# Routing logits placed one unit of work later, and the forms of five experts' weights moved by 3 to 7 work steps

## The chip, the core and the metric

The kernel runs on one core of one Trainium2 chip. The metric is the device time of one execution in microseconds (us); lower is better. Engines are named as in the profile: PE (matmul), PEld (its weight load), DVE (vector), ACT (scalar), POOL (GpSimd) and SP, which here only issues DMAs.

## What is computed

Two blocks follow each other. A sketched attention (batch 4, 4 heads, 1088 tokens, head size 32) gives x with 4352 rows of 128 columns; a mixture of 8 experts, weighted by Sinkhorn routing, works on x:

```python
logits = x @ w_gate                    # 4352 x 8
P = np.exp(logits - logits.max())
for _ in range(8):
    P /= P.sum(1, keepdims=True) + 1e-09
    P /= P.sum(0, keepdims=True) + 1e-09
    P *= N / E
for e in range(E):
    h = np.maximum(x @ w1[e], 0.0)     # 128 -> 1024
    ye = h @ w2[e]                     # 1024 -> 128
    out += P[:, e:e + 1] * ye
```

## The kernel before

**x, in four quarters.** x is kept transposed in `xT`, one quarter of 1088 columns for each batch. The quarter of batch 3 comes last: DVE makes it, `take_over` (L559) writes it to DRAM (`xd`) and reads it back into `xT`, the first 192 of each 288 columns through POOL's DMA queue, the rest through SP's. The last DMAs of both queues are noted in `last_moves`.

**Work steps.** Expert work needs only the quarters that are there, so it starts while attention still runs. `steps()` (L1621) is a generator; each of its steps makes one tile of hidden units (two matmuls, L1147, and their relu on ACT, L1151), issues DVE's differences of older tiles (L1166) and PE's second products (L1601) that are due; tiles are multiplied 8 steps after the first of their block. `fill(n)` (L1713) runs steps until n units are used up; a step costs its columns over 480 units, 416/480 = 0.867 in steps 49 to 96 and 384/480 = 0.8 from 97 on. What stands between two `fill`s in `routing()` (L679) goes to the engines at that place. In this part PE, DVE and ACT run strictly in program order, and all relu tiles, the logits and the small routing products share four PSUM banks in turn (`bank`, L88).

**Routing.** It starts after step 63. `logits(c)` (L573) multiplies the gate with one chunk of columns (512, 288, 288) of all four quarters: four matmuls, each on 32 columns of the PE array, the last for batch 3. `logits_turned` transposes a chunk on DVE, L693 takes the maximum, the matmul L697 turns it, ACT makes the exponentials (L702). Each of eight Sinkhorn iterations is a run of small DVE operations (L708 to L714), one PE product (L718) and two more DVE operations; then `pT` is stored (L730), and weighted sources `xe` and `de` (L862, L876) are made from its parts `px` for the long middle part, which begins at about 199 us.

**Forms.** For experts 1 to 7 the middle part needs sums and differences of quarters of `w1`, made ahead and kept in DRAM as `wl` and `wf`. `forms_ahead(e, area)` (L267) gives nine pieces: 1 five loads on SP, two from DRAM to DRAM (`raw_of_first`, L265) and three into SBUF called d, t3 and z (L279); 2 d is negated on ACT (L282) and a second load is added to it by an accumulating DMA on POOL (L276); 3 the same for t3; 4 the lower half of z is negated; 5 the upper half of z is made on ACT from the summed d; 6 d's lower half is copied out (SP, L279); 7 z is added to d (POOL); 8 two copies out; 9 the last copy out, of the new d. `forms_at` (L595) hangs piece i on the work step that has the number of `passed` at the call plus its i-th figure. Experts 1 and 2 are placed earlier (`forms_of_two`, after step 48) and still have pieces at steps 64 to 75; experts 3 to 7 are placed by `forms_of_five` (L604), after step 63. SP and POOL issue these DMAs in program order, so one that waits holds the later ones.

Groups of columns change after steps 64, 80, 96 and 112; four to eight steps later ACT copies the finished sums out of PSUM (L954 to L971, nine copies).

Of the kernel before, what the change touches and what calls it, by code (L numbers as in the profile page):

```python
# [44 lines left out]
def kernel(  # L45
# [12 lines left out]
    nc = tc.nc  # L58
    P = nc.NUM_PARTITIONS
    B, H, S, D = q.shape  # L60
# [27 lines left out]
    def bank():  # L88
        return aps.tile([P, 512], F32, tag="a", name="a")
# [29 lines left out]
    xT = big.tile([P, N + 2 * 32], F32, name="xT")  # L119
# [132 lines left out]

    fast = {}

    def split(t):

        return t.rearrange("p (k b f) -> p k b f", k=2, b=2)

    def raw_of_first(e):

        w = fast[e][0]
        for out, x in ((w[upper], moe_w1[e][upper]), (split(w)[lower, :, 0], split(moe_w1[e])[lower, :, 0])):
            tc.keep_in_program_order(nc.sync.dma_start(out=out, in_=x))  # L265

    def forms_ahead(e, area):  # L267

        w = split(moe_w1[e])
        fast[e] = [dram.tile([P, F], F32, name=f"{n}{e}") for n in ("wl", "wf")]  # L270
        wl, wf = (split(t) for t in fast[e])
        d, t3, z = (x.rearrange("p (k f) -> p k f", k=2) for x in area)
        t3 = t3[lower]

        def plus(out, x):
            tc.keep_in_program_order(nc.gpsimd.dma_start(out=out, in_=x, accum_op=Alu.add))  # L276

        def copied(queue, out, x):
            tc.keep_in_program_order(queue.dma_start(out=out, in_=x))  # L279

        def turn(out, x):
            nc.scalar.activation(out=out, in_=x, func=Act.Copy, scale=-1.0)  # L282

        def loads():
            if nc.sync in last_moves:
                with tc.issue_after(last_moves.pop(nc.sync).ins):
                    raw_of_first(e)
            else:
                raw_of_first(e)
            copied(nc.sync, d, w[:, :, 0])  # L290
            copied(nc.sync, t3, w[lower, :, 1])
            copied(nc.sync, z[lower], w[upper, :, 1])

        def turn_all():
            turn(area[0], area[0])
            plus(area[0], w[:, :, 1])

        def turn_low():
            turn(area[1][lower], area[1][lower])
            plus(t3, w[upper, :, 1])  # L300

        def turn_lowest():
            turn(area[2][lower], area[2][lower])

        def turn_across():
            turn(area[2][upper], area[0][lower])

        def keep_low():
            copied(nc.sync, wf[lower, :, 0], d[lower])

        def last_sum():
            plus(area[0], area[2])

        def keep_two():
            copied(nc.sync, wl[lower, :, 1], t3)
            copied(nc.sync, wf[upper, :, 0], z[upper])

        def keep_rest():
            copied(nc.sync, wf[:, :, 1], d)

        return loads, turn_all, turn_low, turn_lowest, turn_across, keep_low, last_sum, keep_two, keep_rest

    wd = consts.tile([P, 2, H, R], F32, name="wd")
# [35 lines left out]
    wg = consts.tile([P, 32], F32, name="wg")  # L359
# [197 lines left out]
    last_moves = {}  # L557
# [15 lines left out]
    def logits(c):  # L573
        lo, hi = chunks[c]
        pg = bank()[:, 0:hi - lo]
        for b in range(B):
            nc.tensor.matmul(pg[32 * b:32 * (b + 1)], wg, xT[:, b * S + lo:b * S + hi], start=True, stop=True,
                             tile_position=(0, 32 * b))
        lgs.append((c, pg))

    lgs = []
# [1 line left out]
    def logits_turned():  # L583
        c, pg = lgs.pop(0)
        lo, hi = chunks[c]
        nc.vector.transpose(out=lgp[:, lo // 32:hi // 32, :].rearrange("p a e -> p (a e)"), in_=pg)

    def pieces(t, n):
        t = t.rearrange("p a b -> p (a b)") if len(t.shape) == 3 else t.rearrange("p a b c -> p (a b c)")
        return [t[:, F // 2 * i:F // 2 * (i + 1)] for i in range(n)]  # L590

    v_left = [pieces(t, 2) for t in v_slots]
    ph_left = [pieces(t, 4) for t in phs]

    def forms_at(e, area, *steps_):  # L595
        for at_, do in zip(steps_, forms_ahead(e, area)):
            aside.setdefault(passed[0] + at_, []).append(do)
# [6 lines left out]
    def forms_of_five():  # L604
        kp = pieces(wk.tile([P, (NT + 1) * H, R, R], F32, tag="kp", name="kp", bufs=1), 4)
        r = pieces(rb, 4)
        forms_at(3, [ph_left[0][3], v_left[0][1], kp[0]], 1, 10, 11, 12, 16, 17, 20, 21, 25)
        forms_at(4, kp[1:4], 6, 13, 14, 15, 19, 20, 23, 24, 28)
        forms_at(5, r[0:3], 12, 17, 18, 20, 26, 27, 30, 31, 35)
        forms_at(6, ph_left[1][0:3], 19, 27, 28, 29, 33, 34, 37, 38, 42)  # L610
        forms_at(7, [r[3], ph_left[1][3], v_left[1][0]], 25, 30, 31, 32, 36, 37, 39, 40, 44)

    def attention(b):

# [64 lines left out]
    def routing():  # L679

        forms_of_five()
        yield 5
        logits(0)
        logits(1)
        yield 0.5
        logits_turned()
        logits(2)
        yield 0.5
        logits_turned()
        logits_turned()  # L690
        lg = lgp[:, :, 0:E]
        mx = sk.tile([P, 1], F32, tag="mx", name="mx")
        nc.vector.tensor_reduce(out=mx, in_=lg, axis=AX.XY, op=Alu.max)  # L693
        yield 3
        pm = bank()[:, 0:P]
        for s in range(2):
            nc.tensor.matmul(pm[64 * s:64 * (s + 1)], mx.to_broadcast([P, 64]), ident, start=True, stop=True,  # L697
                             tile_position=(0, 64 * s))
        nc.vector.reduce_max(mx, pm, axis=AX.X)
        nc.vector.tensor_scalar(mx, mx, -1.0, 64 * math.log(2.0), op0=Alu.mult, op1=Alu.add)  # L700
        pw = p2s[0]
        nc.scalar.activation(out=pw[:, :, 0:E], in_=lg, func=Act.Exp, bias=mx[:, 0:1])  # L702

        step = 1.5 * 2.0 ** (23 - 149 + 64)
        nc.vector.tensor_scalar(pw[:, :, 0:E], pw[:, :, 0:E], step, step, op0=Alu.add, op1=Alu.subtract)
        for it in range(ITERS):
            rs = sk.tile([P, SA], F32, tag="rs", name="rs")
            nc.vector.reduce_sum(rs, pw, axis=AX.X)  # L708
            nc.vector.reciprocal(rs, rs)
            p1 = p1s[it % 2]  # L710
            nc.vector.scalar_tensor_tensor(p1[:, 0:SA], rs.unsqueeze(2).to_broadcast([P, SA, E]), UP,
                                           pw[:, :, 0:E], op0=Alu.mult, op1=Alu.mult)
            cs = sk.tile([P, E], F32, tag="cs", name="cs")
            nc.vector.reduce_sum(cs, p1.rearrange("p g e -> p e g"), axis=AX.X)  # L714
            yield 4.25
            pc = bank()[:, 0:E]
            for s in range(2):
                nc.tensor.matmul(pc[64 * s:64 * (s + 1)], ones[:, 0:64], cs, start=True, stop=True,  # L718
                                 tile_position=(0, 64 * s))
            cr = sk.tile([P, E], F32, tag="cr", name="cr")  # L720
            nc.vector.reciprocal(cr, pc)
            last = it == ITERS - 1
            pw = lgp if last else p2s[(it + 1) % 2]
            nc.vector.scalar_tensor_tensor(pw[:, :, 0:E], cr.unsqueeze(1).to_broadcast([P, SA, E]),
                                           float(N) / E * (1.0 if last else UP), p1[:, 0:SA],
                                           op0=Alu.mult, op1=Alu.mult)

        nc.vector.transpose(out=lgT.rearrange("p a s -> p (a s)"), in_=lgp.rearrange("p a e -> p (a e)"))
        for b in (1, 0, 2, 3):
            tc.keep_in_program_order((nc.gpsimd if b != 1 else nc.sync).dma_start(  # L730
                out=pT[:, b * S:(b + 1) * S], in_=lgT[32 * b:32 * b + E].rearrange("p a s -> p (a s)")))
# [564 lines left out]
    def middle():  # L1296
# [149 lines left out]
        def second_product(k, i, row):  # L1446
# [3 lines left out]
            for w, x, *place in products[k][i]:  # L1450
# [9 lines left out]
                if op is not None:  # L1460
                    tc.add_manual_dep(mm.ins, op, SYNC, reason="row tiles of one bank")
            waited[1 - row].discard(bank_)
# [1 line left out]

        products, witnesses, issued, waited = {}, [(0, last_relu[0])], [], (set(), set())
        written = {(i, row): -1 for i in range(4) for row in range(2)}
        SYNC = mybir.DependencyInfo(mybir.DependencyClass.Sync, mybir.DependencyReason.DATA)
        number = {}

        def witness(k, p, n, ins):  # L1470
# [18 lines left out]
        for n, k in enumerate(ks):  # L1489
# [3 lines left out]
            g, e = items[j]  # L1493
# [326 lines left out]
```

## Time and profile before

| what | value |
|---|---|
| three runs | 886.57, 886.80, 888.33 us; median 886.8 |
| the profiled execution | 886.74 us |
| its span, first to last instruction | 885.0 us, so 1.74 us lie around it |
| busy: PE, DVE, ACT, POOL | 876.4, 792.2, 570.7, 176.6 us |
| granted PE clock | 0.999 |
| DMA | 174.67 MB, mean 197 GB/s |

The times of the trace are counted from the first instruction. A row of the timeline gives start, length, engine, line, operation, output and inputs, how many instructions were merged (x4), and in brackets how long the engine was idle before and what ended that. SPq rows are DMA issues, not transfers.

### The profile page before, as it was taken

How to read it: one execution, taken by the hardware profiler on the slowest of the kernel's cores; microseconds unless marked ns; L12 is line 12 of the kernel's file. 1: busy time of each engine (PE TensorE's matmuls, PEld its weight loads, DVE VectorE, ACT ScalarE, POOL GpSimd, SP SyncE). 2: the span in 40 equal slices, each digit the busy share in tenths (PEclk: the TensorE clock that was granted, in tenths of full speed). 3: DMA queues.
4: the chain of work that ended last, by engine and by line, in shares of the span. 5: the costliest groups of instructions: out<-in, count | busy, mean ns of one | idle time of the engine just before them, and what ended most of it. 6: DMA issues, size and time to landing. Idle time of an engine off the chain costs nothing.

```text
span 885.0 us, 28699 instructions
## 1 busy us (share of the span) xinstructions
PE 876.4 (99%) x11790; PEld 628.1 (71%) x11790; DVE 792.2 (90%) x1628; ACT 570.7 (64%) x1309; POOL 176.6 (20%) x244
## 2 busy tenths in 40 slices
PE   9999999999999999999999999999999999999997
PEld 6777544454777777777777777888778777776665
DVE  7678778978999999999999999899998999998875
ACT  3356577678666677667676766676766666755643
POOL 3121333120211221222122211231122122200000
PEclk9999999999999999999999999999999999999999
DMA  9998799475877877877786777697568776774340
GB/s 258 305 278 276 160 228 213 108 180 176 235 220 208 244 217 205 235 185 209 197 240 172 212 212 191 168 241 219 173 165 227 212 226 179 208 203 97 94 106 13
DMA packets 97459, 174.67 MB, mean 197 GB/s; under 512 B 29216, under 2 KB 68976, under 8 KB 92480
## 3 DMA queue, kind: packets, MB, share of 16 engines
q1 hardware_dynamic: 74832, 139.67, 49.9%
q0 software_dynamic: 21264, 33.00, 21.6%
q8 instruction: 93, 1.52, 0.7%
q10 hardware_dynamic: 1232, 0.16, 0.1%
q14 instruction: 38, 0.31, 0.1%
HBM read 125.70 MB, written 25.08 MB: 170 GB/s over the span
## 4 chain that ended last, share of the span: by engine, by line
PE 90%; DVE 6%; ACT 1%; DMA 1%; issue 1%; SPq 0%; DVEq 0%; POOL 0%; POOLq 0%
PE s L1601 39%; PE a L1313 37%; PE a L1147 10%; DVE hb L1166 2%; PE a L421 1%; DVE hb L1215 1%; PE a L536 1%; PE a L108 1%; DMA xT<-xd 0%; PE a L388 0%; DVE hx L1215 0%; DVE ws L238 0%; PE s L450 0%; DMA xd<-xt 0%; ACT hb L1151 0%
## 5 line engine op out<-in xcount | busy, mean ns | idle before, releaser
L1313 PE MATMUL a<-xe,w 64*64 64x384 f32 x2164 | 418.1, 484 | 0.0
L1601 PE MATMUL s<-hb,ws 64*64 64x256 f32 (+4 forms) x2962 | 381.8, 384 | 1.1 <-DVE hb L1166 0.9
L1601 PE MATMUL s<-hx,ws 64*64 64x256 f32 (+1 forms) x2894 | 349.3, 376 | 0.1
L1313 PE MATMUL a<-de,w 64*64 64x384 f32 x1600 | 309.4, 483 | 0.0
L1601 PEld LDWEIGHTS s<-hb,ws 64*64 64x64 f32 (+1 forms) x2962 | 202.7, 133 | 73.7 <-issue 23.8
L1601 PEld LDWEIGHTS s<-hx,ws 64*64 64x64 f32 (+1 forms) x2894 | 196.9, 133 | 56.1 <-issue 10.2
L1215 DVE TENSOR_TENSOR hb<-hb 128x512 f32<-128x512 f32 (+1 forms) x340 | 187.7, 578 | 1.4 <-ACT hb L1348 1.1
L1313 PEld LDWEIGHTS a<-xe,w 64*64 64x64 f32 x2164 | 147.3, 133 | 25.4 <-issue 2.0
L1348 ACT ACTIVATE hx<-a 128x384 f32<-128x384 f32 x204 | 97.0, 492 | 63.9 <-PE a L1313 62.1
L1348 ACT ACTIVATE hb<-a 128x384 f32<-128x384 f32 x204 | 97.6, 492 | 59.5 <-PE a L1313 57.7
L1147 PE MATMUL a<-xT,w 128*64 128x256 f32 (+3 forms) x576 | 130.6, 453 | 0.4 <-ACT hb L1151 0.4
L1313 PEld LDWEIGHTS a<-de,w 64*64 64x64 f32 x1600 | 111.4, 133 | 19.2 <-ACT hb L1348 0.6
L1215 DVE TENSOR_TENSOR hx<-hx 128x512 f32<-128x512 f32 (+1 forms) x204 | 118.3, 595 | 0.0
L876 POOL DMA_DIRECT2D de<-xe x68 | 56.9, 984 | 295.2 <-ACT de L869 169.7
L1151 ACT ACTIVATE hb<-a 128x256 f32<-128x256 f32 (+3 forms) x148 | 66.6, 453 | 54.8 <-PE a L1147 44.5
L1344 ACT ACTIVATE hb<-a 128x384 f32<-128x384 f32 x136 | 66.7, 491 | 33.1 <-PE a L1313 31.9
L1353 DVE TENSOR_TENSOR a<-a,hb 128x384 f32<-128x384 f32 x136 | 76.7, 564 | 11.2 <-PE a L1313 7.0
L1342 ACT COPY a<-a 128x384 f32<-128x384 f32 x136 | 63.1, 464 | 31.5 <-PE a L1313 30.9
L1166 DVE TENSOR_TENSOR hb<-hb 128x416 f32<-128x416 f32 (+7 forms) x90 | 60.8, 675 | 21.2 <-ACT hb L1151 18.5
L1147 PEld LDWEIGHTS a<-xT,w 128*64 128x64 f32 x576 | 55.7, 137 | 28.0 <-issue 16.1
L1601 PE MATMUL s<-hb,w 128*64 128x256 f32 (+3 forms) x280 | 69.6, 435 | 0.0
L876 POOL DMA_DIRECT2D de<-de x34 | 29.6, 872 | 135.0 <-issue 78.1
(226 smaller groups left out, 1020.2 us busy)
## 6 DMA issues: line engine op xcount, KB each, us to landing
ws<-ws SPq DMA_DIRECT2D x34, 1280.0 KB, 6.5
w<-wl SPq DMA_DIRECT2D x34, 512.0 KB, 7.7
w<-wf SPq DMA_DIRECT2D x33, 512.0 KB, 8.3
px<-pT SPq DMA_DIRECT2D x34, 384.0 KB, 9.3
w<-in_moe_w_dram SPq DMA_DIRECT2D x16, 512.0 KB, 4.5
de<-xe POOLq DMA_DIRECT2D x34, 192.0 KB, 3.1
de<-de POOLq DMA_DIRECT2D x34, 192.0 KB, 8.1
ws<-in_moe_w_dram SPq DMA_DIRECT2D x7, 512.0 KB, 7.8
```

The costliest lines, as they stand in the source:

```text
L108: nc.tensor.matmul(warm[:, 0:P], ones, ones, start=True, stop=True)
L876: tc.keep_in_program_order(nc.gpsimd.dma_start(out=out, in_=x, accum_op=Alu.add))
L1147: nc.tensor.matmul(ph[sl], loaded_w[j][0][:, P * f + H2 * s:P * f + H2 * (s + 1)], sources[j][:, lo:hi], start=True, stop=True, tile_posit ...
L1151: last_relu[:] = [nc.scalar.activation(out=out, in_=ph, func=Act.Relu).ins.name]
L1166: nc.vector.tensor_tensor(out, a, b, op=Alu.subtract)
L1215: nc.vector.tensor_tensor(places(out), places(a), places(b), op=Alu.subtract if off else Alu.add)
L1313: nc.tensor.matmul(out[sl], w[r, c0 + H2 * s:c0 + H2 * (s + 1)], x[r], start=start, stop=stop, tile_position=(H2 * row, H2 * s), skip_grou ...
L1342: witness(k, p, 1, nc.scalar.copy(b, bx))
L1344: witness(k, p, 5, nc.scalar.activation(out=m5s[p], in_=b, func=Act.Copy, scale=1.0 if p else -1.0))
L1348: ins = nc.scalar.activation(out=out, in_=x, func=Act.Relu)
L1353: ins = nc.vector.tensor_tensor(by if what == 1 else raw(k, p, 1, 1), bb[p], m5s[p], op=Alu.add)
L1601: mm = nc.tensor.matmul(sums[g][i][H2 * s:H2 * (s + 1), n * place:n * (place + 1)], w, x, start=c == (2 if t == 3 and row is None else 1) ...
```

## The change

Three edits. `routing()` yields 6 units instead of 5 before the first two logits, and 2.25 instead of 3 before the maximum is turned. The last matmul of `logits(0)` is noted in `all_there`, and the first load of forms issued after it (expert 3's) waits for it by an added semaphore dependency. The five lines of `forms_of_five` have other steps. What was tied behind the last move of `xT` on SP was expert 3's first load; now it is the first copy out that SP issues for the forms after that move.

```diff
 in raw_of_first(e):
-            tc.keep_in_program_order(nc.sync.dma_start(out=out, in_=x))
+            ins = tc.keep_in_program_order(nc.sync.dma_start(out=out, in_=x))
+            if all_there:
+                tc.add_manual_dep(ins.ins, all_there.pop(), SYNC, reason="behind the last x")
 in forms_ahead:
         def copied(queue, out, x):
-            tc.keep_in_program_order(queue.dma_start(out=out, in_=x))
+            if queue in last_moves:
+                with tc.issue_after(last_moves.pop(queue).ins):
+                    queue.dma_start(out=out, in_=x)
+            else:
+                tc.keep_in_program_order(queue.dma_start(out=out, in_=x))
         def loads():
-            if nc.sync in last_moves:
-                with tc.issue_after(last_moves.pop(nc.sync).ins):
-                    raw_of_first(e)
-            else:
-                raw_of_first(e)
+            raw_of_first(e)
 in logits(c):
+        if c == 0:
+            all_there.append(mm.ins.name)
 in forms_of_five:
-        forms_at(3, [...], 1, 10, 11, 12, 16, 17, 20, 21, 25)
-        forms_at(4, [...], 6, 13, 14, 15, 19, 20, 23, 24, 28)
-        forms_at(5, [...], 12, 17, 18, 20, 26, 27, 30, 31, 35)
-        forms_at(6, [...], 19, 27, 28, 29, 33, 34, 37, 38, 42)
-        forms_at(7, [...], 25, 30, 31, 32, 36, 37, 39, 40, 44)
+        forms_at(3, [...], 8, 13, 14, 15, 19, 20, 23, 24, 28)
+        forms_at(4, [...], 11, 16, 17, 18, 26, 27, 30, 31, 35)
+        forms_at(5, [...], 15, 20, 21, 27, 31, 32, 35, 36, 40)
+        forms_at(6, [...], 20, 28, 29, 30, 34, 35, 38, 39, 43)
+        forms_at(7, [...], 26, 32, 33, 35, 42, 43, 46, 47, 50)
 in routing:
-        yield 5
+        yield 6
         logits(0)
         logits(1)
 ...
-        yield 3
+        yield 2.25
         pm = bank()[:, 0:P]
```

Counting the units gives the places, as the number of steps done:

| what | before | after |
|---|---|---|
| logits 0 and 1 | 69 | 70 |
| logits 2, first chunk turned | 70 | 71 |
| other chunks turned, maximum | 70 | 72 |
| maximum turned by PE, exponentials | 74 | 74 |
| products of the eight iterations | 79, 84, 89, 93, 99, 104, 109, 114 | 79, 84, 89, 94, 99, 104, 109, 115 |
| pieces 1 to 9 of expert 3 | 64, 73, 74, 75, 79, 80, 83, 84, 88 | 71, 76, 77, 78, 82, 83, 86, 87, 91 |
| of expert 4 | 69, 76, 77, 78, 82, 83, 86, 87, 91 | 74, 79, 80, 81, 89, 90, 93, 94, 98 |
| of expert 5 | 75, 80, 81, 83, 89, 90, 93, 94, 98 | 78, 83, 84, 90, 94, 95, 98, 99, 103 |
| of expert 6 | 82, 90, 91, 92, 96, 97, 100, 101, 105 | 83, 91, 92, 93, 97, 98, 101, 102, 106 |
| of expert 7 | 88, 93, 94, 95, 99, 100, 102, 103, 107 | 89, 95, 96, 98, 105, 106, 109, 110, 113 |

Left as they are: expert 1's pieces 7, 8, 9 at steps 64, 65, 69, and expert 2's pieces 5 to 9 at 66, 67, 70, 71, 75.

More of the change, by code (lines that the diff above doesn't have):

```diff
@@ L251, in store_four @@
         tc.keep_in_program_order(nc.sync.dma_start(out=stored_four[e], in_=ws))
-    fast = {}
+    fast, all_there = {}, []
+    SYNC = mybir.DependencyInfo(mybir.DependencyClass.Sync, mybir.DependencyReason.DATA)
     def split(t):
@@ L576, in logits @@
         for b in range(B):
-            nc.tensor.matmul(pg[32 * b:32 * (b + 1)], wg, xT[:, b * S + lo:b * S + hi], start=True, stop=True,
-                             tile_position=(0, 32 * b))
+            mm = nc.tensor.matmul(pg[32 * b:32 * (b + 1)], wg, xT[:, b * S + lo:b * S + hi], start=True, stop=True,
+                                  tile_position=(0, 32 * b))
+        if c == 0:
+            all_there.append(mm.ins.name)
         lgs.append((c, pg))
@@ L606, in forms_of_five @@
         r = pieces(rb, 4)
[L607 to L611, printed above, removed]
+        forms_at(3, [ph_left[0][3], v_left[0][1], kp[0]], 8, 13, 14, 15, 19, 20, 23, 24, 28)
+        forms_at(4, kp[1:4], 11, 16, 17, 18, 26, 27, 30, 31, 35)
+        forms_at(5, r[0:3], 15, 20, 21, 27, 31, 32, 35, 36, 40)
+        forms_at(6, ph_left[1][0:3], 20, 28, 29, 30, 34, 35, 38, 39, 43)
+        forms_at(7, [r[3], ph_left[1][3], v_left[1][0]], 26, 32, 33, 35, 42, 43, 46, 47, 50)
     def attention(b):
@@ L1466, in middle @@
         written = {(i, row): -1 for i in range(4) for row in range(2)}
-        SYNC = mybir.DependencyInfo(mybir.DependencyClass.Sync, mybir.DependencyReason.DATA)
         number = {}
```

## Prediction

> **What bounds the kernel now.** First the page's head, then the waits of PE over the whole run.
>
> ```profile
> span 885.0 us, 28699 instructions
> PE 876.4 (99%) x11790; PEld 628.1 (71%) x11790; DVE 792.2 (90%) x1628; ACT 570.7 (64%) x1309; POOL 176.6 (20%) x244
> PE 90%; DVE 6%; ACT 1%; DMA 1%; issue 1%; SPq 0%; DVEq 0%; POOL 0%; POOLq 0%
> ```
> ```profile
> PE s L1601 <- DVE hb L1166: 0.9, 2, 0.7
> PE a L577 <- DMA xT<-xd: 0.7, 1, 0.7
> PE a L1147 <- ACT hb L1151: 0.4, 1, 0.4
> ```
>
> PE is busy for 876.4 of 885.0 us and owns 90% of the chain. The change issues the same PE products, so it can only win or lose in PE's waits. Three of the kinds of wait fall where the edits are, 2.0 us of idle PE together. I then read PE's timeline around them.
>
> ```profile
> 106.10 1.06 PE L577 MATMUL a<-xT,wg 128*32 128x512 f32 x6
> 107.81 1.50 PE L577 MATMUL a<-xT,wg 128*32 128x512 f32 x10 [0.66 <-DMA xT<-xd]
> 109.25 0.92 PE L1147 MATMUL a<-xT,w 128*64 128x416 f32 x4
> 110.00 0.87 PE L1601 MATMUL s<-hb,w 128*64 128x416 f32 x4
> 110.80 0.69 PE L577 MATMUL a<-xT,wg 128*32 128x288 f32 x8
> 111.42 0.92 PE L1147 MATMUL a<-xT,w 128*64 128x416 f32 x4
> ...
> 113.56 0.51 PE L1601 MATMUL s<-hb,ws 128*64 128x416 f32 x1
> ...
> 113.91 0.51 PE L1601 MATMUL s<-hb,ws 128*64 128x416 f32 x1
> ```
> ```profile
> 130.63 0.92 PE L1147 MATMUL a<-xT,w 128*64 128x416 f32 x4 [0.43 <-ACT hb L1151]
> 142.85 0.56 PE L1601 MATMUL s<-hb,ws 128*64 128x416 f32 x1 [0.71 <-DVE hb L1166]
> ```
>
> The reader is to see that an idle time understates its loss. A matmul of 416 columns is shown 0.51 long, but the next starts 0.35 after it; what the two overlap, 0.16, is lost as well when PE has to wait. **Wait A**, the logits: three quarters ran (x6, two records each), the fourth waited for its part of xT, and the two chunks filled 106.10 to 109.25, 3.15 us. Chunk 2, with all four quarters side by side, took 110.80 to 111.42, 0.62 for 288 columns; at that rate 512 + 288 columns take 1.72. The loss is 1.43, twice the idle. **Wait B** (130.63): 0.43 + 0.16 less a little pipeline, 0.55. **Wait C** (142.85): 0.71 + 0.16 = 0.87.
>
> What is behind B and C stands in the timelines of ACT, SP, POOL and DVE:
>
> ```profile
> 128.63 0.63 ACT L282 ACTIVATE rb<-rb 128x512 f32<-128x512 f32 x1 [3.46 <-DMA rb<-in_moe_w_dram]
> 129.16 0.50 ACT L1151 ACTIVATE hb<-a 128x416 f32<-128x416 f32 x1
> ...
> 133.11 0.51 ACT L954 COPY z<-s 64x416 f32<-64x416 f32 x1
> ...
> 137.31 0.52 ACT L1151 ACTIVATE hb<-a 128x416 f32<-128x416 f32 x1
> ```
> ```profile
> 109.07 0.56 SPq L279 DMA_DIRECT2D wf<-ph  x1
> ...
> 114.28 6.26 SPq L279 DMA_DIRECT2D wf<-ph  x2
> 120.59 1.50 SPq L265 DMA_DIRECT2D wl<-in_moe_w_dram  x2
> ```
> ```profile
> 112.57 0.85 POOL L276 DMA_DIRECT2D ph<-ph  x1 [8.49 <-PE a L1147]
> ```
> ```profile
> 137.85 1.02 DVE L1166 TENSOR_TENSOR hb<-hb 128x832 f32<-128x832 f32 x1 [1.49 <-ACT hb L1151]
> ...
> 139.53 0.21 DVE L721 RECIPROCAL cr<-a 128x8 f32<-128x8 f32 x1
> ...
> 142.22 1.21 DVE L1166 TENSOR_TENSOR hb<-hb 128x416 f32<-128x416 f32 x2
> ```
>
> Read backwards. B: ACT stood 3.46 us at expert 5's first negation (after step 80) because its load came late: SP issued expert 5's loads only from 120.59, held from 114.28 by expert 2's last copy out. That waited for POOL's sum at 112.57, which overwrites what SP copied out at 109.07, behind five loads of expert 3 in the same queue. (PE is named there; it had long been done, so I take the copy's landing.) C: ACT, behind since then, runs without a gap from 129.16 through the nine copies of a change of groups; the relu at 137.31 releases DVE's difference at 137.85, and a Sinkhorn run stands in front of the next one, at 142.22, for which PE waits.
>
> **The change part by part.** Everything is against the profiled execution: 885.0 + 1.74 around it = 886.74, the median being 886.8.
>
> *Logits after step 70.* The 70th step, 109.25 to 110.80 in the rows above, goes ahead of them. It carries PE from 106.10 to 107.50 or 107.65 (four matmuls of 0.35, or the 1.55 of those rows with a restart in it). From the chain and SP's timeline:
>
> ```profile
> 102.02 1.75 SPq L562 DMA_DIRECT2D xT<-xd  x4
> 103.81 1.32 SPq L265 DMA_DIRECT2D wl<-in_moe_w_dram  x2
> ```
> ```profile
> 103.33 4.35 DMA xT<-xd
> ```
>
> The last part of xT landed at 103.33 + 4.35 = 107.68, so at most 0.2 of the wait is left, and the quarters run side by side again. I take 1.35 gained (ends 1.2 and 1.65, the latter if both chunks pass as fast as three quarters of chunk 0 did in 1.06).
>
> *The wait on SP, and the copies that pass it.* Behind the last xT now come expert 1's and 2's copies out (pieces 8, 6, 9, 8), then expert 3's loads, which wait for logits 0 (about 108.7). Behind that wait stand loads for experts 3, 4, 5, and behind these ACT's negations and POOL's sums. Piece 9 of expert 1 waits anyway, for a POOL sum:
>
> ```profile
> 102.74 1.34 POOL L276 DMA_DIRECT2D kx<-v  x1
> ```
> ```profile
> kx<-v POOLq DMA_DIRECT2D x1, 256.0 KB, 6.2
> ph<-in_moe_w_dram SPq DMA_DIRECT2D x1, 256.0 KB, 5.0
> ```
>
> 102.74 + 6.2 = 108.9, so the added wait costs nothing beside it. Without that cover SP would be free at about 106 (three issues after 103.81) and stand still until 108.7; these 3 us would come off the room that follows. With some 0.65 an issue, expert 3's d leaves at about 111.6 and lands at 116.6; its negation, after step 76, is due at about 118.5. Room 2 us, where before it was 6. Expert 2's copy (109.07 before) leaves at about 105, POOL's sum follows at 109 instead of 112.57, SP isn't held at 114.28, and expert 5's loads leave near 118 instead of 120.59. Their negation stands after step 83, three steps of 1.3 later. B's cause is gone: +0.55 (ends 0, if a load is late again, and 0.55).
>
> *Steps of the negations.* Each is 0.63 on ACT and stands between two relus of 0.5, in a step of 1.3 (15 matmuls of 0.35 in four steps): it fits, except among the nine copies after steps 85 to 88. There none stands, as before; one comes right ahead of them (84). Without the backlog the copies start about 0.6 earlier against PE than at 133.11, and the relu, DVE's difference and the Sinkhorn run with them. I take 0.6 of C's 0.87 as gone (ends 0 and 0.87); what is late next is the same DVE difference, whose second wait (two times, 0.9 in all, so 0.2) stays. Four kinds of DMA move along; POOL's order keeps each sum behind its negation.
>
> *Routing.* The last chunks are turned after step 72 and the maximum is used after 74, as before; DVE needs about 1 us for them, two steps are 2.6: nothing. The last product comes a step (1.3) later, so `px` and what hangs on it do:
>
> ```profile
> 178.31 0.81 SPq L832 DMA_DIRECT2D px<-pT  x2
> ```
> ```profile
> 184.81 0.56 DVE L862 TENSOR_TENSOR xe<-xT,px 128x384 f32<-128x384 f32 x1 [0.17 <-DMA px<-pT]
> ```
> ```profile
> 194.99 0.87 POOL L876 DMA_DIRECT2D de<-de  x1 [5.54 <-DMA de<-xe]
> ```
> ```profile
> de<-de POOLq DMA_DIRECT2D x1, 192.0 KB, 3.0
> ```
> ```profile
> 199.64 2.08 PE a L1313 x16
> ```
>
> DVE already waits 0.17 for it. The chain runs on to the `de` sum, 194.99 + 3.0 = 198.0, and PE's first new product is at 199.64: 1.3 later still fits, and this room of 1.6 is the cover. Cost 0 (ends 0 and 1.3, if nothing of it holds).
>
> **Sum**: 1.35 + 0.55 + 0.6 = 2.5; 886.74 - 2.5 = 884.2.
>
> **A rule weighed.** The Trainium skill, page "DMA: Bandwidth & Descriptors", section "Queues, rings and completion order", says that a DMA engine takes queues in turn, packet by packet, but consumes one queue's descriptors in ring order. By this, loads queued behind xT on SP's own queue hardly delay it, and holding them back wins nothing at A; only POOL's traffic competes. The trace has xT's last part at 4.35 with both behind it, and can't part them. By the rule the landing stays at 107.68; without it, it might be 1 earlier. The sum is 884.4 by the rule (the 0.2 of A stays) and 884.2 without.
>
> **The rivals.**
> - *Waits move into ACT.* Expert 3's and 4's loads are now close together with expert 5's, with 2 us of room. Against it: ACT may stand nearly 3 us before PE feels it (3.46 cost 0.55). For it: C needs only a late start of the copies. Then B and C come back and A's gain stays: 886.74 - 1.35 = 885.4.
> - *xT lands later*, as four copies out now follow it at once: if the fourth quarter lands 1.4 later, A stays whole at its new place, and only B and C go: 886.74 - 1.15 = 885.6. For it: the last part already took 4.35 us; against it: what follows them stands behind them in the same queue.
> - *Slower.* Experts 3 to 5 miss their steps: the place is ACT's queue at steps 76 to 84, deciding when a load lands over 3 us after its step, which takes loads of 8 us instead of 5. One such wait cost B + C = 1.4; three cost 4.2, less A's 1.35: 889.6.
> - *Nothing*: the edits don't reach the waits (SP was held by something else, and A's fourth quarter waits at its new place as long): 886.7.
>
> **How the numbers follow.** Forecast 884.2, own range 883.2 (all of A's 1.65, B, C and some of the rest) to 885.0: 0.66. Waits in ACT 0.12, xT later 0.07, nothing 0.05, slower 0.10. A measurement of this kernel can tell about 0.2%, 1.8 us, so the line is at 885.0: faster 0.67, within 0.22, slower 0.11. The range to 886.3 takes in the forecast and the two partial rivals.
>
> **What would show it.** Right: the timeline of the logits as one block of some 1.6 us with no DMA wait above 0.2; expert 5's negation without a DMA wait; PE's waits between 100 and 170 under 0.7 us. Wrong: a wait of ACT L282 for a DMA at steps 76 to 84; a PE wait near 199 for `de` or `xe`; wait C as long as before.

## The result, and the profile after

| | before | after |
|---|---|---|
| median of 9 runs each | 887.34 us (885.89 to 888.33) | 884.58 us (883.27 to 885.75) |
| ratio | | 0.9972, 95% interval 0.9962 to 0.9982 |
| profiled execution, its span | 886.74, 885.0 us | 885.55, 883.8 us |

The kernel became 0.28% faster by the ratio, some 2.5 us (the two medians are 2.76 apart); 884.2 was forecast. The profiled execution of after lies near the upper end of its nine; where it lost time is said below. Its lines are 1 to 7 higher in number: the tile matmul is L1152, its relu L1156, DVE's difference L1171, the logits L580, ACT's negation L289.

PE's waits, whole run, in the profile of after (who waited, for whom: us, times, longest):

```profile
PE a L108 <- POOL own L110: 1.0, 1, 1.0
PE s L1605 <- DMA ws<-ws: 0.7, 1, 0.7
PE s L1605 <- DVE hb L1171: 0.7, 2, 0.6
PE a L469 <- ACT kvz L439: 0.6, 1, 0.6
PE a L503 <- DVE rd L554: 0.4, 1, 0.4
PE s L1605 <- DVE hx L1358: 0.2, 1, 0.2
```

The rows for `xT` (0.7) and for ACT (0.4) of before are gone, DVE's has shrunk from 0.9 to 0.7. Two rows are new, 0.7 and 0.4; they lie at 549 and at 38 us, where nothing was edited. PE's timeline of after around the logits, and at the wait that is left:

```profile
106.67 0.92 PE L1152 MATMUL a<-xT,w 128*64 128x416 f32 x4
107.36 0.92 PE L1605 MATMUL s<-hb,w 128*64 128x416 f32 x4
108.22 1.55 PE L580 MATMUL a<-xT,wg 128*32 128x512 f32 x16
109.70 0.92 PE L1152 MATMUL a<-xT,w 128*64 128x416 f32 x4
```
```profile
141.16 0.56 PE L1605 MATMUL s<-hb,ws 128*64 128x416 f32 x1 [0.57 <-DVE hb L1171]
```

The 70th step now stands ahead of the logits; both chunks are one row of 16 records, 108.22 to 109.70, 1.48 us instead of 3.15. ACT's timeline of after at expert 5's negation:

```profile
128.40 0.63 ACT L289 ACTIVATE kp<-ph 64x512 f32<-64x512 f32 x1 [1.41 <-DMA ph<-in_moe_w_dram]
129.06 0.52 ACT L1156 ACTIVATE hb<-a 128x416 f32<-128x416 f32 x1
129.47 0.62 ACT L289 ACTIVATE rb<-rb 128x512 f32<-128x512 f32 x1
```

The `rb` row, which had 3.46 us of waiting in front of it, has none. A new wait of 1.41 stands ahead: expert 3's fifth piece, after step 82, for a sum of POOL's. SP and POOL, of after:

```profile
110.24 0.56 SPq L286 DMA_DIRECT2D wl<-ph  x1
...
111.55 1.85 SPq L266 DMA_DIRECT2D wl<-in_moe_w_dram  x2
...
119.64 1.25 SPq L266 DMA_DIRECT2D wl<-in_moe_w_dram  x2
120.94 1.99 SPq L286 DMA_DIRECT2D rb<-in_moe_w_dram  x3
```
```profile
110.82 0.85 POOL L279 DMA_DIRECT2D ph<-ph  x1 [5.49 <-DMA wf<-ph]
```

SP isn't held for 6 us at 114 any more, yet expert 5's `rb` loads leave at 120.94, against 122.13 before. That is 1.2 us earlier, or 1.9 if both are counted from the start of step 69; the first of them took 7.88 us to land instead of 6.47, so that it landed at 128.81, against 128.60 before.

**A ledger by work steps.** A step has four records of the tile matmul, so the n-th step begins with record 4(n-1)+1 of that line in PE's timeline. For step 100 these are the rows of before and of after:

```profile
151.55 0.52 PE L1147 MATMUL a<-xT,w 128*64 128x384 f32 x1
```
```profile
149.64 0.52 PE L1152 MATMUL a<-xT,w 128*64 128x384 f32 x1
```

From the 69th step (104.55 before, 105.27 after) these are 47.00 and 44.37 us: 2.63 us are won inside this stretch. The span shows 1.19, because after began the stretch 0.72 late and waited 0.75 at 549. The ledger keeps what happens outside of the stretch apart from the edits, and is used below:

| us between first products | 69 to 73 (logits) | 84 to 86 (expert 5) | 93 to 96 (Sinkhorn) | 96 to 100 (expert 7) | 69 to 100 |
|---|---|---|---|---|---|
| before | 9.02 | 3.51 | 5.24 | 5.04 | 47.00 |
| before, again | 7.35 | 4.94 | 5.24 | 5.04 | 46.76 |
| after | 7.35 | 2.90 | 5.10 | 4.82 | 44.37 |
| after, again | 7.35 | 2.90 | 4.57 | 4.82 | 43.84 |
| logits only | 7.35 | 5.37 | 5.23 | 4.82 | 46.97 |
| forms only | 8.14 | 2.90 | 4.56 | 5.03 | 44.83 |
| no wait on SP | 7.35 | 2.90 | 5.33 | 4.82 | 44.60 |
| expert 3's loads first | 7.36 | 2.90 | 4.57 | 4.82 | 43.84 |
| expert 5's negation early | 7.35 | 7.29 | 4.57 | 4.82 | 49.81 |
| Sinkhorn run later | 7.35 | 2.90 | 4.31 | 4.81 | 43.58 |
| expert 5 alone | 7.81 | 2.90 | 4.82 | 6.95 | 46.67 |
| expert 5, one step | 7.55 | 2.90 | 5.29 | 6.01 | 45.96 |
| expert 5 and logits | 7.35 | 2.90 | 5.05 | 7.96 | 47.47 |
| experts 5, 7 and logits | 7.66 | 2.90 | 4.57 | 4.82 | 44.15 |

Steps 73 to 84 take 15.00 us in every one of these profiles, steps 86 to 93 take 9.19 to 9.20 in all but one. Each row is one profiled execution. For two kernels it was among the slower ones of that kernel (expert 5 alone 889.29 us, its median 886.37; expert 5 and logits 886.98, its median 885.42), so these rows need not be typical.

### The profile page after: what moved, and what is told of

Its sections match the earlier page's. It is cut to its first block, busy times and chain, and to the rows that moved or that the text cites. A ratio compares the mean times of both kernels' runs of the same rounds, so it can differ in the third digit from the quotient of the medians.

```text
span 883.8 us, 28694 instructions
## 1 busy us (share of the span) xinstructions
PE 875.3 (99%) x11790; PEld 631.7 (71%) x11790; DVE 792.7 (90%) x1628; ACT 571.1 (65%) x1309; POOL 176.5 (20%) x244
## 4 chain that ended last, share of the span: by engine, by line
PE 91%; DVE 5%; DMA 2%; ACT 1%; issue 1%; DVEq 0%
PE s L1605 40%; PE a L1318 36%; PE a L1152 12%; DMA qx<-in_q_dram 1%; DMA ws<-ws 1%; PE a L424 1%; DVE hb L1220 1%; PE a L539 1%; DVE hb L1171 1%; PE a L391 0%; PE s L453 0%; DVE hx L1220 0%; DVE ws L238 0%; DMA raw<-in_S_dram 0%; PE a L503 0%
## 5 line engine op out<-in xcount | busy, mean ns | idle before, releaser
L1605 PEld LDWEIGHTS s<-hb,ws 64*64 64x64 f32 (+1 forms) x2962 | 201.4, 133 | 71.5 <-issue 24.1
L1152 PE MATMUL a<-xT,w 128*64 128x256 f32 (+3 forms) x576 | 129.9, 453 | 0.0
L1156 ACT ACTIVATE hb<-a 128x256 f32<-128x256 f32 (+3 forms) x148 | 67.0, 454 | 55.7 <-PE a L1152 43.8
L1171 DVE TENSOR_TENSOR hb<-hb 128x416 f32<-128x416 f32 (+7 forms) x90 | 61.3, 681 | 16.3 <-ACT hb L1156 13.0
L1152 PEld LDWEIGHTS a<-xT,w 128*64 128x64 f32 x576 | 55.5, 137 | 27.9 <-issue 15.5
```

The lines of the kernel that those rows point to most:

```text
L1152: nc.tensor.matmul(ph[sl], loaded_w[j][0][:, P * f + H2 * s:P * f + H2 * (s + 1)], sources[j][:, lo:hi], start=True, stop=True, tile_posit ...
L1156: last_relu[:] = [nc.scalar.activation(out=out, in_=ph, func=Act.Relu).ins.name]
L1171: nc.vector.tensor_tensor(out, a, b, op=Alu.subtract)
L1605: mm = nc.tensor.matmul(sums[g][i][H2 * s:H2 * (s + 1), n * place:n * (place + 1)], w, x, start=c == (2 if t == 3 and row is None else 1) ...
```

## The experiments

**After, again.** The same kernel, a single run.

> The changed kernel once more, for what one profile can vary. Between the first product of work step 69 and that of step 100 the profile of before needs 47.00 us on PE (104.55 to 151.55) and the one of after 44.37 (105.27 to 149.64). My theory, that the gain lies in this stretch alone: 44.2 to 44.6 again, while the waits outside of it (0.36 us at 38, 0.75 us at 549 in the profile of after) may come or go. Rival, that part of the 2.6 us is chance: the stretch differs from 44.37 by 0.5 us or more.

Measured: 43.84 us from step 69 to 100, 0.5 less than in the first profile, all of it at steps 93 to 96; neither of the waits at 38 and 549 us came back. By the mark set ahead, 0.5 us of the stretch is chance. The first, second and fourth columns repeat to 0.01 us in this kernel; the Sinkhorn column differs between two profiles of one kernel, and what it follows is said below.

**Logits only.** The kernel before with

```diff
-        yield 5
+        yield 6
...
-        yield 3
+        yield 2.25
```

> Only the yields are changed (6 and 2.25); forms, their steps and the order on SP as before. My theory: the wait in the logits goes (step 69 to 73 on PE 7.4 to 7.6 us instead of 9.02), but PE and ACT are then 1.6 us earlier against expert 5's load, which is set by the DMA queues; ACT waits some 5 us there instead of 3.46, the wait of PE on ACT grows from 0.4 to about 2 us, and step 73 to 88 takes 22 to 23 us instead of 21.30. In all 0 to 0.6 us faster than before. Rival, the edits add up independently: step 73 to 88 stays at 21.3 and the kernel is 1.6 us faster.

Ratio 0.9997 (0.998 to 1.0014). The logits' 1.67 us are won, and lost again 11 steps later (5.37 instead of 3.51). ACT's and PE's timelines of this kernel:

```profile
129.26 0.63 ACT L282 ACTIVATE rb<-rb 128x512 f32<-128x512 f32 x1 [5.32 <-DMA rb<-in_moe_w_dram]
```
```profile
130.34 0.29 PE L718 MATMUL a<-cs,ones 128*64 128x8 f32 x4 [1.45 <-ACT hb L1151]
131.26 0.92 PE L1147 MATMUL a<-xT,w 128*64 128x416 f32 x4 [0.62 <-ACT hb L1151]
```

Expert 5's load lands at nearly the same time as before (129.23 against 128.60, where this profile began the stretch 0.43 late), PE and ACT arrive 1.7 us earlier and wait for it so much longer. Another 1.27 us went behind the ledger's end (steps 100 to 115 took 20.34 us, 19.07 before), after ACT had stood 3.33 us at 155.93 for the summed d of expert 7. The rival, that the edits add up, is out by the ledger; the interval of the ratio just reaches its 1.6 us.

**Forms only.** The changed kernel with yields 5 and 3.

> Only the forms are changed (steps, order, wait); the yields are 5 and 3 as before. By the ring-order theory (DMAs queued behind xT on the same queue don't delay it): the last part of xT takes 4.3 us as before, the logits wait as before, step 69 to 73 takes about 9.0 us, and only some 0.9 us of the other two waits is won. By the contention theory (expert 3's loads behind xT slow its landing; in the profile of after its last part took 3.0 us instead of 4.35): the fourth quarter is there within 0.3 us of the logits, step 69 to 73 takes 7.4 to 7.8 us, and the kernel is 2 us or more faster than before, nearly as fast as with all edits.

Ratio 0.997 (0.9956 to 0.9985), as fast as all edits together by the comparison. In the ledger the logits lose 0.79 of the 1.67, which fits neither theory: xT's last part took 3.42 us here. What it takes in the other kernels tells more. With expert 3's loads behind it on SP: 4.35, 2.79 (both before), 3.26, 3.32, 2.91, 2.70, 4.43, 3.21; without: 3.03, 3.13 (both after), 3.42, 3.35, 3.17, 3.35. The medians are 3.24 and 3.26, so the loads behind don't slow it as a rule; two of eight are over 4 with them and none of six without, which is too few to tell chance from cause.

**No wait on SP.** The changed kernel with

```diff
-            if all_there:
-                tc.add_manual_dep(ins.ins, all_there.pop(), SYNC, reason="behind the last x")
```

> The changed kernel without the added semaphore wait; order and steps as changed. My theory: SP reaches expert 3's first load at 111.55 anyway, after the logits (which end at about 109.7), held by POOL's sum for expert 1 and three copies, so nothing changes: step 69 to 100 takes 44.2 to 44.6 us, the ratio to the kernel before is 0.997. Rival, the wait matters: expert 3's loads leave earlier, the logits wait again, 0.5 us or more is lost.

Ratio 0.9954 (0.9935 to 0.9972), 44.60 us in the ledger: nothing is lost without it. In the profile of after SP waited 0.5 us for the logits at this place, behind 3.2 us for expert 1's sum:

```profile
SPq L286 <- DMA kx<-v: 3.2, 1, 3.2
...
SPq L266 <- PE a L580: 0.5, 1, 0.5
```

**Expert 3's loads first.** Yields and all steps as changed, no wait, but:

```diff
-        forms_at(3, [...], 8, 13, 14, 15, 19, 20, 23, 24, 28)
+        forms_at(3, [...], 1, 13, 14, 15, 19, 20, 23, 24, 28)
```

> The logits and all steps as changed, but expert 3's loads back at step 64, so that SP issues them right behind xT and ahead of the copies for experts 1 and 2, and no added wait. If the order on SP is what removed the wait of PE on ACT (the prediction's reason): SP is held again until about 120, expert 5's load lands near 128.6 and PE waits again; step 84 to 86 takes 3.4 us or more instead of 2.91. If the later step of the negation (83 instead of 80) removed it: ACT waits under 1.5 us for that load, step 84 to 86 stays at 2.9 to 3.0, and the kernel is as fast as the changed one (0.996 to 0.998 of before). The fourth quarter's last DMA, with loads behind it again: 4 us and more if they slow it, 3.0 to 3.5 if not.

Ratio 0.9953 (0.9937 to 0.997), 43.84 us, and step 84 to 86 at 2.90. SP was held as in before; its `rb` loads left at 123.52 in a stretch that began 1.48 late, and ACT had to wait 0.17 us for them, its timeline:

```profile
129.33 0.63 ACT L282 ACTIVATE rb<-rb 128x512 f32<-128x512 f32 x1 [0.17 <-DMA rb<-in_moe_w_dram]
```

The order on SP, the reason that the prediction gave, isn't needed.

**Expert 5's negation early.** The changed kernel with

```diff
-        forms_at(5, r[0:3], 15, 20, 21, 27, 31, 32, 35, 36, 40)
+        forms_at(5, r[0:3], 15, 17, 18, 20, 31, 32, 35, 36, 40)
```

> The changed kernel with three pieces of expert 5 alone (its negations) back at steps 80, 81, 83; its loads stay at step 78, order on SP as changed. If the step of the negation matters: its load lands near 128.8 as in the profile of after, ACT waits for it 5 us and more from about 123, step 84 to 86 takes 4.8 us or more instead of 2.91, and the gain is gone but for some tenths (ratio 0.999 to 1.001). If the order on SP is enough: ACT waits under 3 us and step 84 to 86 stays below 3.1.

Ratio 1.0006 (0.9992 to 1.002): these three figures undo the whole gain, with SP's order as changed (ACT's wait alone is not all of it, see below). ACT and PE of this kernel:

```profile
129.78 0.63 ACT L289 ACTIVATE rb<-rb 128x512 f32<-128x512 f32 x1 [4.83 <-DMA rb<-in_moe_w_dram]
```
```profile
130.87 0.29 PE L723 MATMUL a<-cs,ones 128*64 128x8 f32 x4 [1.47 <-ACT hb L1156]
132.30 1.65 PE L1152 MATMUL a<-xT,w 128*64 128x416 f32 x4 [1.15 <-ACT hb L1156]
```

The matmuls right after are stretched, 1.65 us instead of 0.92. The trace gives the reason: the granted clock was 0.5 from 131.46 to 138.29, after PE had done no more than four short matmuls between 129.39 and 132.30. The clock row of this kernel's page shows it in one slice:

```profile
PEclk9999998999999999999999999999999999999999
```

Half of these 6.83 us, 3.4, is my estimate of what that cost, in steps 84 to 86 and 86 to 93 (10.77 instead of 9.19). The ledger without it would be some 46.4, still 2.0 above after and near the two of before. Six of the ten runs had a mean clock of 0.995 to 0.998. The other four have a median of 888.05, against 887.63 of the eighteen runs of before at 0.999 and more, so the gain is gone without the lower clock too.

**Sinkhorn run later.** The changed kernel with

```diff
-            yield 4.25
+            yield {2: 5.0, 3: 3.5}.get(it, 4.25)
```

> The changed kernel with one Sinkhorn product, and the run of DVE operations behind it, after step 90 instead of 89 (the two iterations' yields are 5.0 and 3.5 instead of 4.25 and 4.25). My theory of the third wait: the run stands ahead of DVE's two differences that PE needs, and copies that start late push all of it. With the run behind them the wait is gone whatever the DMAs do: step 93 to 96 takes 4.5 to 4.6 us (before 5.24, after 5.10, its repeat 4.57), PE waits for DVE at L1171 under 0.3 us in all, and the kernel is 0.3 us faster than the changed one at most, which the comparison can't show. Rival: ACT's copies alone decide, and the wait stays in some profiles.

Steps 93 to 96 take 4.31 us, the least of all, and the wait there is gone; but steps 100 to 115 took 19.43 instead of 18.98, with a new wait of 0.2 for DVE at 161, so the stretch to the first product of the middle part is 92.05 us against 92.39 and 91.85 of the two profiles of after. Ratio 0.9958 (0.9943 to 0.9973), no different. It moves the wait rather than removing it.

**Before, again.** A single run, 886.82 us.

> The kernel before once more, for what one profile of it can vary. My theory: the three waits come back, the first with 0.8 to 1.7 us of loss by the landing of xT's last part (step 69 to 73 takes 8.1 to 9.1 us), the second and third together 1.0 to 2.0 us; step 69 to 100 takes 46 to 47.5 us (47.00 in the first profile). Rival: the first profile was a chance draw, and this one is within 0.5 us of the 44.4 of the changed kernel.

46.76 us instead of 47.00, and by other waits: the 8.1 to 9.1 us expected at the logits were 7.35. PE's and ACT's timelines of this repeat:

```profile
106.55 1.55 PE L577 MATMUL a<-xT,wg 128*32 128x512 f32 x16
```
```profile
128.84 0.63 ACT L282 ACTIVATE rb<-rb 128x512 f32<-128x512 f32 x1 [4.89 <-DMA rb<-in_moe_w_dram]
```

xT's last part came after 2.79 us, the unchanged logits ran as one block without a wait; and the 1.67 us that were not lost there went into ACT's wait (4.89 instead of 3.46) and into steps 84 to 86 (4.94 instead of 3.51). The wait in the logits, from which the largest term of the sum came, wasn't what bound the kernel in this run.

**Expert 5 alone.** The kernel before with

```diff
-        forms_at(5, r[0:3], 12, 17, 18, 20, 26, 27, 30, 31, 35)
+        forms_at(5, r[0:3], 12, 20, 21, 27, 31, 32, 35, 36, 40)
```

> The kernel before with one line changed: expert 5's loads stay at step 75, its negations go to steps 83, 84 and 90 and its later pieces to 94, 95, 98, 99 and 103, as in the changed kernel. Logits, order on SP and all other steps as before. My theory by now: the load of expert 5 lands some 24 us after the first product of step 69 whatever is done to the logits or to SP's order, and ACT's wait for it is what bounds this stretch; moving the negation is enough. ACT waits under 2 us for it, step 84 to 86 takes 2.9 to 3.1 us, step 69 to 73 takes 7.35 to 9.1 (as xT lands), and the ratio is 0.995 to 0.998. Rival, the prediction's sum (order on SP and logits each needed): step 84 to 86 stays at 3.4 or more and the ratio is 0.998 or above.

A miss: ratio 0.9994 (0.9981 to 1.0008). Step 84 to 86 is at 2.90 as expected, but the kernel isn't faster. ACT's timeline shows what is late next, expert 7's negation after step 93 (its d lies in `rb` too). First the row of before for it, then two rows of this kernel:

```profile
143.88 0.63 ACT L282 ACTIVATE rb<-rb 128x512 f32<-128x512 f32 x1 [0.53 <-DMA rb<-in_moe_w_dram]
```
```profile
130.39 0.63 ACT L282 ACTIVATE rb<-rb 128x512 f32<-128x512 f32 x1 [0.79 <-DMA rb<-in_moe_w_dram]
147.81 0.63 ACT L282 ACTIVATE rb<-rb 128x512 f32<-128x512 f32 x1 [5.19 <-DMA rb<-in_moe_w_dram]
```

The wait isn't longer only because ACT comes earlier. Expert 7's load left SP 35.0 us after the start of step 69, much as before (35.4, in the repeat 35.3), but took 6.78 us to land instead of 3.92 and 4.25. In all eleven profiles of kernels in which expert 5's pieces 5 to 9 come later it took 6.2 to 8.8 us, in the three others 3.9 to 4.3. So in this profile expert 7's load landed later as well, 41.8 us after the start of step 69 instead of 39.3 and 39.5; why isn't shown. Expert 5's negations alone, with its pieces 5 to 9 left where they were, were not run.

**Expert 5, one step.** As the one before, with 12, 18, 19, 21 for the first four figures.

> As the kernel before, but expert 5's negations one step later (81, 82, 84) instead of three; its later pieces as in the one before this. My theory, by the two profiles of before (ACT waited 3.46 us where the logits lost 1.67, and 4.89 where they lost nothing, and step 84 to 86 took 3.51 and 4.94): a step is 1.3 us, so ACT waits 2.2 us and step 84 to 86 takes 2.9 to 3.1 if the logits lose, or 3.5 us and 3.4 to 3.9 if they don't. Rival, the wait isn't a matter of that step: as before, 3.5 or 4.9.

The logits lost 0.2 here, ACT waited 1.95 us, and step 84 to 86 took 2.90: one step was enough in this profile, where the load landed 22.5 us after the start of step 69, against 24.1 in the first profile of before. With so little lost at the logits, 3.5 us of waiting were expected; the early landing made it 1.95. Expert 7's wait was 4.74, steps 96 to 100 took 6.01.

**Expert 5 and logits.** Expert 5's line and the yields 6 and 2.25.

> The same one line for expert 5, and the yields 6 and 2.25; all other steps, the order on SP and the missing wait as before. My theory: this is all of the change that counts. Step 69 to 73 takes 7.35, step 84 to 86 2.9 to 3.1, step 69 to 100 43.8 to 45.0 us, ratio 0.995 to 0.998, no different from the changed kernel. Rival, the other experts' steps are needed: a new wait of ACT for expert 6's or 7's loads, PE waits of 0.5 us and more between 130 and 170.

A miss in its size: ratio 0.9983 (0.9968 to 0.9999), 47.47 us in the ledger. The rival had it: another expert's step is needed, expert 7's. With nothing lost ahead of it, its wait is the longest yet, and its load took 7.48 us here. The comparison (some 1.5 us faster) and this profile's ledger (0.5 to 0.7 slower than the two of before) disagree; the six quickest of the twelve runs, 884.52 to 885.32, are as fast as the changed kernel, so the loss at expert 7 probably varies from run to run, which no second profile shows. ACT's and PE's timelines:

```profile
147.46 0.63 ACT L282 ACTIVATE rb<-rb 128x512 f32<-128x512 f32 x1 [6.07 <-DMA rb<-in_moe_w_dram]
```
```profile
148.55 0.87 PE L1147 MATMUL a<-xT,w 128*64 128x384 f32 x4 [2.24 <-ACT hb L1151]
```

**Experts 5, 7 and logits.** The last kernel and

```diff
-        forms_at(7, [...], 25, 30, 31, 32, 36, 37, 39, 40, 44)
+        forms_at(7, [...], 25, 32, 33, 35, 42, 43, 46, 47, 50)
```

> The yields 6 and 2.25, expert 5's line as in the two kernels before (loads at 75), and expert 7's negations at 95, 96 and 98 and its later pieces at 105, 106, 109, 110 and 113 as in the changed kernel (loads stay at 88). Experts 3, 4 and 6, the order on SP and the missing wait as before. My theory, corrected: three late things stand in a row (the last part of xT, expert 5's load, expert 7's load), each hides the next, and a gain at one is given back at the next. ACT waited 6.07 us for expert 7's load with its negation at step 93; two steps of 1.3 later it waits about 3.5, PE loses 0.5 at most, the four steps 96 to 100 take 4.8 to 5.4 us instead of 7.96, step 69 to 100 takes 44.0 to 45.3, and the ratio is 0.995 to 0.998. Rival, the order on SP or the steps of experts 3, 4 and 6 are needed too: another wait of ACT for a DMA takes the place of it, step 69 to 100 stays above 46 us and the ratio above 0.998.

Ratio 0.9971 (0.9961 to 0.9982), 44.15 us in the ledger (xT's last part took 4.43 us here, so that 0.31 was lost at the logits even after step 70). ACT's timeline and PE's waits from 100 to 200 us, in this kernel:

```profile
146.07 0.63 ACT L282 ACTIVATE rb<-rb 128x512 f32<-128x512 f32 x1 [1.64 <-DMA rb<-in_moe_w_dram]
```
```profile
PE s L1601 <- DVE hb L1166: 0.2, 1, 0.2
```

Two yields, two lines of steps: that is as fast as the whole change, without the wait, the order on SP and the steps of experts 3, 4 and 6. It is no faster; no kernel here is shown to beat the changed one. The two lines without the yields were not run; that the forms without the yields (above) reach 0.997 leaves open whether the yields are needed at all.

## Why the prediction was right, and where it was not

The time, the sign and the range were right, and the sum of 2.5 us stands against 2.63 in the ledger. That the sum agrees to 0.1 us is in part luck: one term came out 0.32 larger and one 0.46 smaller than taken, and 0.22 us were won at expert 7, which had no term. The causes given for the terms were partly wrong.

1. *The logits* (1.35 taken, ends 1.2 and 1.65): the loss was 1.67, at the upper end, and the edit removes it. But the step from "The loss is 1.43, twice the idle" to "I take 1.35 gained" failed: it is no term that can be added. Alone the edit shows no gain (0.9997, with 0.998 to 1.0014), and the unedited kernel reaches the same time without that loss (886.82 and 886.74). PE's time here was set by expert 5's load, which landed 22.5 to 24.4 us after the start of step 69 in all 14 profiles, whatever was edited; the logits' loss lay in its shadow. In the changed kernel, where the later waits are gone, the edit is worth what xT's landing costs: 0.79 us in the one profile without it, 0 to 1.7 by the others.
2. *Expert 5's wait* (0.55): it went, 3.51 to 2.90, 0.61. The step that failed is its reason: "SP isn't held at 114.28, and expert 5's loads leave near 118 instead of 120.59". The first of its five left at 119.64 and `rb` at 120.94, which landed at 128.81, as at 128.60 before. The loads early on SP in the old order do as well (2.90), the negation at the old step with the new order does not (ratio 1.0006, part of it the lower clock). What counts is the step of the negation. The prediction had named that too, as a side remark.
3. *The Sinkhorn wait* (0.6 of 0.87): 0.14 in one profile, 0.67 in its repeat. The column follows what ACT waits for DMAs between 118 and 134 us, ahead of the copies: with 0 to 0.7 us steps 93 to 96 take 4.56 or 4.57 (four profiles), with 0.79 4.82, with 1.02 5.05, with 1.41 and more 5.10 to 5.33 (six). Two profiles are left out, the one with the lower clock and the one with the later Sinkhorn run. That fits the mechanism, copies that start late, and by it the new wait of ACT for expert 3's sum, 1.41, kept it alive in the first profile. A wait of ACT for a DMA at steps 76 to 84 was the prediction's own sign of being wrong; this is the rival "waits move into ACT", in part.
4. *Not seen:* expert 7's negation. Its negations moved by two steps or three, and without that the profiles lose again at steps 96 to 100 what the other edits won (6.95 and 7.96 instead of 4.82). The trace of before shows a wait of 0.53 us there, which the prediction doesn't name; it was short because ACT came late, and because the load took 3.92 us and not the 6.78 and 7.48 of these two.
5. *Costs put at nothing*: the wait on SP (0.5 us of SP, nothing in time) and the later last product (DVE waits 0.18 for `px`, the middle part begins 1.91 earlier as everything does) held. Ring order, as the Trainium skill's page "DMA: Bandwidth & Descriptors", section "Queues, rings and completion order", has it, is not contradicted: medians 3.24 with and 3.26 without loads behind.
6. *The slower rival* had the right mechanism: ACT behind a load that is over 3 us late. It wasn't the changed kernel but its parts that ran into it, at expert 5 and at expert 7.

In short: three late arrivals stand in a row, xT's last part, expert 5's load and expert 7's load, and what PE doesn't lose at one it loses at the next. The change moves PE's need behind all three. That they add up was wrong, and the sum came out because all three were edited at once. What stays open is whether expert 7's load would be late if expert 5's later pieces had stayed.

## What to carry to other kernels

A wait that the trace shows is worth its length only if nothing later is tied to a time of its own: ask for each later DMA on the way how long its engine waited, and how much longer it would wait if the work came earlier by what you mean to win. Waits that PE doesn't feel today are the next bound. Compare two profiles by the starts of the same work steps rather than by their spans: in two profiles of one kernel three of the four stretches agreed to 0.01 us, and the fourth differed by 0.53, where the spans differed by 1.6. One profile is one draw: set its time against the other runs of its kernel before you read a loss from it.

## What the runs showed of the hardware

- In this kernel, with its four PSUM banks in turn, ACT could be about 2.9 us late before PE lost anything: waits of ACT of 3.46, 4.89 and 5.32 us cost PE 0.61, 2.04 and 2.47 at steps 84 to 86, and 1.95 cost nothing. For expert 7, 4.74, 5.19 and 6.07 cost 1.19, 2.13 and 3.14, so 2.9 to 3.6 us were free there.
- The same 48 KB transfer took 2.70 to 4.43 us from issue to landing in 14 profiles of kernels that were alike up to it (what was queued behind it differed).
- Some profiles hold a wait of PE for a `ws` load near 550 us (0.75 in after, 0.4, 0.9 and 1.8 in three others, none in the repeats), where nothing was edited; single times differ by up to 1.8 us for it.
- In one profile a long wait of PE was followed by a lower clock. In the kernel with expert 5's negation early, the granted clock fell to 0.5 for 6.83 us after PE had all but stood still for 2.9 us; no other profile shows less than the full clock between 8 and 879 us. A mean clock under 0.999 is on record for 13 of the 85 runs of before that the experiments were compared with (median 889.31 us, the others 887.27), for 6 of 10, 3 of 12 and 2 of 12 runs of "expert 5's negation early", "logits only" and "expert 5 and logits", and for none of the 66 runs in the comparisons of the changed kernel and of the six other kernels. Whether it was PE's waits in those runs too isn't shown: only one of them was profiled.
